# Preparation steps of a three-part kernel: two products between a transfer and its first step, up to five or six steps after a product, twelve working tiles

## Chip, core and metric

The kernel runs on one core of a Trainium2 chip. The metric is the device time of one execution in microseconds (us). The engines are TensorE (PE, with its weight loads PEld), VectorE (DVE), ScalarE (ACT), GpSimd (POOL) and SyncE (SP), whose queue issues the DMA transfers.

## What is computed

Attention over 4 batches, 8 heads, 576 positions and head size 64 gives 2304 tokens of width 512. Two layers with an inner width of 1536 follow; the inputs are fp32, and the weights reach the kernel as 64-bit words.

```python
q_p = phi(q)                                    # phi(x) = max(x, exp(x) - 1) + 1
mem_out = (q_p @ M_prev) / (q_p . z_prev + 1e-6)
local = softmax(causal(q @ k.T * scale)) @ v
g = 1 / (1 + exp(-beta))
x = (g * mem_out + (1 - g) * local)             # -> [2304, 512]
gate = 1 / (1 + exp(-(x @ w_gate)))             # layer 0
x = (gate * (x @ w_val)) @ w_out
out = ((x @ w_a) * (x @ w_b)) @ w_out2          # layer 1
```

## The kernel before

**Products.** Each fp32 operand is split into a rounded high part and a low part. A product is three TensorE passes, high·high, high·low and low·high (`mm3`, L447 to L452; in `out_rows` of layer 1, L1178 to L1180). Tokens form four blocks of 512 columns (0 to 3) and one short block of 256 (block `B` = 4). The inner width is 12 chunks of 128 columns, `c`.

**Order of the work.** Attention takes the first 337 us. Block 3 and the short block then pass through the first four chunks (`early`: per chunk a gate product `tg`, a value product `tv`, `gate()`, and an out product in `flush`). After it, for each layer, the pairs of chunks in `PAIRS` (4 in layer 0, 6 in layer 1): `group(layer, g, 0)`, `plain` (the short block), `group(layer, g, 1)`; then `outs(layer)`. A group multiplies two chunks with two blocks in seven products instead of eight, in the order 1, 2, 6, 5, 7, 3, 4. Each is 12 matmuls of 128x512 for each of two kinds of weights, in two PSUM banks. Three products add into banks of an earlier one, after ACT has copied these out (`keep`, L1038): product 6 into those of 1, product 7 into those of 6, product 3 into those of 5. In this part PE runs in the order in which the code is written; a scheduler orders the other engines.

**Preparation.** After each product `hook(rate)` raises the count of turns and gives up to `rate` steps to the first `WIN` unfinished tasks of one list (`steps`). A step starts only if its working tiles (`t`, NT of 128x512), staging buffers (`s`, NS of 512 KB) and units (NL and NH places for finished operands) are free. The tasks are:

- `piece`: load one chunk of weights into staging `st` (SP, L815/L819); two ACT steps that scale (L827, L828); two DVE steps that shift and merge (L830, L833); a POOL add into `wt` (L838), which frees the staging; then, unless the chunk is mixed first, the high part on ACT (L806) and the low part on DVE or POOL (L800);
- `mix` and `convert`: sums of two chunks, then their high and low parts;
- `x_mixed` and `x_plain`: the same for the tokens of two blocks, or of the short one.

In `outs`, `g_split` loads one block and chunk of the gated product back (L1159) and splits it on ACT (L1161) and DVE or POOL (L1162), three blocks and chunks ahead of its product. In `early`, `gate()` multiplies on DVE (L531), rounds on ACT (`gh`, L148) and subtracts on DVE (`gl`, L538).

Of the kernel before, what the change touches and what calls it, by code (L numbers as in the profile page):

```python
# [13 lines left out]
I32 = mybir.dt.int32  # L14
# [5 lines left out]
def kernel(  # L20
# [17 lines left out]
    P = 128  # L38
# [490 lines left out]
    def gate(vps, s, n, tag="g"):  # L529

        st["gate"] = vec.tensor_tensor(  # L531
            out=s[:, 0:n], in0=vps[:, 0:n], in1=s[:, 0:n], op=ALU.mult
        )
        te = (dict(tag="gh", bufs=NG), dict(tag="gl", bufs=NG)) if NE is None else 2 * (dict(tag="e", bufs=NE),)
        gh = work.tile([P, 512], F32R, name="gh", **te[0])
        gl = work.tile([P, 512], F32R, name="gl", **te[1])
        rnd(gh[:, 0:n], s[:, 0:n], "g" in CD)
        (pool if NE is None else vec).tensor_tensor(  # L538
            out=gl[:, 0:n], in0=s[:, 0:n], in1=gh[:, 0:n].bitcast(F32), op=ALU.subtract
        )  # L540
        return gh, gl
# [197 lines left out]
    with tc.manual_schedule(engines={mybir.EngineType.PE}):  # L739
# [3 lines left out]
        work = bctx.enter_context(tc.tile_pool(name="workb", bufs=2))  # L743
        NL, NH, NE, NT, NS = 15, 10, 7, 10, 2
        wl = bctx.enter_context(tc.tile_pool(name="wl", bufs=NL))
# [31 lines left out]

        def units_left(half):
            return sum(h[2] - h[1] for h in homes if half in (h[3], "A"))

# [28 lines left out]
        def piece(layer, c, kind, half, mixed, on_pool):  # L809
            yield (0, 0, 1)  # L810
            free["s"] -= 1
            s = stp.tile([P, 512, 2], I32, tag="st", name="st")
            w32 = src[layer][kind].bitcast(I32)
# [4 lines left out]
            else:  # L818
# [3 lines left out]
                )  # L822
            yield (0, 1, 0)
            hi, lo = s[:, :, 1], s[:, :, 0]
# [11 lines left out]
            )  # L836
            yield (0, 0, 0)
            pool.tensor_tensor(out=c32, in0=c32, in1=lo, op=ALU.add)  # L838
            freed.append("s")
            if mixed:  # L840
# [46 lines left out]
        def x_mixed(layer, sb, j):  # L887
# [14 lines left out]

            yield ("L", 0, 0)
            high(1, a11)
# [30 lines left out]
        def x_plain(layer):  # L935
# [24 lines left out]

            yield ("L", 0, 0)
            a = [high(kk) for kk in (0, 1)]
# [10 lines left out]
        def task(gen, when=None):  # L973
            tasks.append([gen, None, when])

        def advance(x):
            x[1] = next(x[0], False)
            if x[1] is False:
                tasks.remove(x)

        WIN = 5

        def steps(k):

            starved, seen = False, 0
            for x in list(tasks):
                if x[2] is not None:
                    if not x[2]():
                        starved = True
                        continue  # L990
                    x[2] = None
                seen += 1
                if not k or seen > WIN:
                    break
                if x[1] is None:
                    x[1] = next(x[0])
                u, t, s = x[1]
                if starved and (u or t):
                    continue
                if u and not units_left(u) or t > free["t"] or s > free["s"]:  # L1000
                    starved = True
                    continue
                advance(x)
                k -= 1
# [12 lines left out]
        def need(f):  # L1017

            for n in range(200):
                if f():  # L1020
                    return
                hook(3)
            raise AssertionError(f"no progress {units_left()} {free} {[(x[0].__name__, x[0].gi_frame.f_locals.get('layer'), x[0].gi_frame.f_locals.get('sb'), x[0].gi_frame.f_locals.get('c'), x[0].gi_frame.f_locals.get('kind'), x[1]) for x in tasks[:10]]}")

# [106 lines left out]
        def plain(layer, g, rate):  # L1131

            n = cols(B)
            last_g = g == PAIRS[layer][-1][0]
            for c in (g, g + MATE[layer]):
                need(lambda: (layer, KD - 1) in x4 and all((layer, c, k) in ws for k in H2))
                o = []
# [17 lines left out]
        def g_split(layer, blk, c):  # L1155
# [5 lines left out]
            act.activation(out=t[:, 0, 0:n], in_=f, func=AF.Copy)  # L1161
            (vec if c % 2 and not layer else pool).tensor_tensor(  # L1162
                out=t[:, 1, 0:n], in0=f, in1=t[:, 0, 0:n].bitcast(F32), op=ALU.subtract
# [22 lines left out]
        def outs(layer, rate):  # L1186
# [3 lines left out]
            for m, (blk, c) in enumerate(seq):  # L1190
                while ahead < min(m + 4, len(seq)):
                    settle_free()
                    key = (layer, seq[ahead][1], 2)
                    need(lambda: key in ws and units_left(half_of(ws[key])))
                    g_split(layer, *seq[ahead])
                    ahead += 1
# [117 lines left out]
        for c in upper:  # L1314
            task(piece(0, c, 2, "A", False, False))
        wave(1, 0, False)
# [7 lines left out]
        for c in every:  # L1324
            task(piece(1, c, 2, "A", False, False))

        ends = []
        early(B - 1, 3)
        early(B, 3)
        for layer in H2:  # L1330
            for g, h in PAIRS[layer]:
                group(layer, g, 0, 3)
                plain(layer, g, 3)
                group(layer, g, 1, 3)
            outs(layer, 3)
        bctx.close()
# [31 lines left out]
```

## Time and profile before

| | before |
|---|---|
| median of 3 runs | 1119.66 us (1119.29 to 1122.21) |
| profiled execution | 1121.79 us, span 1120.0 us |
| PE, DVE, ACT, POOL busy | 95%, 55%, 50%, 44% |

The profile is of one execution; its times count from the start of the span. Busy shares are means over the span. In brackets a row gives the idle time of the engine before it and what ended that. PEclk is the TensorE clock that was granted, as a share of full speed (2.4 GHz).

### The profile page before, as it was taken

What the parts mean: (1) busy time and instruction counts of PE and PEld (TensorE: products, weight loads), DVE (VectorE), ACT (ScalarE), POOL (GpSimd) and SP (SyncE); (2) the same over time, 40 slices, a digit from 0 to 9 for tenths busy, and PEclk for the clock granted to TensorE, in tenths of its full rate; (3) what the DMA queues carried; (4) which work ended last, traced back from release to release, by engine and by line L of the source; (5) the groups of instructions that cost most, each with busy time, mean ns of one, the idle gap of its engine ahead of it and who ended that gap; (6) DMA issues with size and microseconds to landing.
All of it is one profiled execution on the core that took longest, in us unless ns stands there. A gap on an engine that the chain in (4) does not pass through costs nothing. (4 is left out here: it accounts for less than half of the span.)

```text
span 1120.0 us, 16371 instructions
## 1 busy us (share of the span) xinstructions
PE 1065.5 (95%) x5624; PEld 848.9 (76%) x5624; DVE 616.8 (55%) x1179; ACT 557.3 (50%) x1173; POOL 492.2 (44%) x432
## 2 busy tenths in 40 slices
PE   5888999999999889999999999989999999989998
PEld 3556677777777777888888878768888888868886
DVE  3888755555434785456459574956555455550000
ACT  4877766666644454454555342534344444442221
POOL 1566552242121553444446451643453444764542
PEclk8999999999999999999999999989999999999999
DMA  6565533323114333323248756313323323742343
GB/s 148 135 166 152 141 92 105 82 69 101 41 67 124 107 110 122 104 85 132 79 157 291 239 197 221 113 58 122 112 87 123 107 82 132 245 142 89 107 137 100
DMA packets 147204, 140.63 MB, mean 126 GB/s; under 512 B 73776, under 2 KB 107696, under 8 KB 147120
## 3 DMA queue, kind: packets, MB, share of 16 engines
q1 hardware_dynamic: 147120, 139.58, 39.5%
q8 instruction: 44, 0.72, 0.3%
q14 instruction: 40, 0.33, 0.1%
HBM read 97.00 MB, written 42.54 MB: 125 GB/s over the span
## 5 line engine op out<-in xcount | busy, mean ns | idle before, releaser
L450 PE MATMUL gv<-xm,w 128*128 128x512 f32 (+1 forms) x752 | 275.0, 366 | 3.5 <-DVE w L800 3.5
L448 PE MATMUL gv<-xm,w 128*128 128x512 f32 (+1 forms) x752 | 274.8, 365 | 3.6 <-ACT ev L1038 3.6
L449 PE MATMUL gv<-xm,w 128*128 128x512 f32 (+1 forms) x752 | 274.6, 365 | 0.0
L448 PEld LDWEIGHTS gv<-xm,w 128*128 128x128 f32 x752 | 143.1, 190 | 27.8 <-ACT ev L1038 4.9
L450 PEld LDWEIGHTS gv<-xm,w 128*128 128x128 f32 x752 | 142.9, 190 | 26.6 <-DVE w L800 4.0
L449 PEld LDWEIGHTS gv<-xm,w 128*128 128x128 f32 x752 | 143.1, 190 | 22.8
L1038 ACT ACTIVATE ev<-gv 128x512 f32<-128x512 f32 (+1 forms) x168 | 92.7, 562 | 127.7 <-PE gv L450 127.4
L1042 DVE TENSOR_TENSOR ev<-gv,ev 128x512 f32<-128x512 f32 x120 | 82.2, 689 | 119.1 <-PE gv L450 87.2
L1162 POOL TENSOR_TENSOR gs<-ev,gs 128x512 fp32r<-128x512 f32 (+1 forms) x80 | 99.8, 1263 | 96.3 <-ACT gs L1161 96.1
L1047 POOL TENSOR_TENSOR ev<-ev 128x512 f32<-128x512 f32 x60 | 84.9, 1415 | 127.9 <-DVE ev L1042 52.2
L838 POOL TENSOR_TENSOR wt<-wt,st 128x512 int32<-128x512 int32 x60 | 84.6, 1417 | 92.8 <-DVE wt L833 67.8
L1161 ACT ACTIVATE gs<-ev 128x512 fp32r<-128x512 f32 (+1 forms) x100 | 55.8, 583 | 89.5 <-DMA ev<-gd 65.1
L1180 PE MATMUL gv<-w,gs 128*128 128x512 f32 x216 | 85.4, 395 | 2.9 <-POOL gs L1162 2.9
L1179 PE MATMUL gv<-w,gs 128*128 128x512 f32 x216 | 85.1, 394 | 0.8 <-DVE w L800 0.8
L1178 PE MATMUL gv<-w,gs 128*128 128x512 f32 x216 | 84.8, 392 | 0.1
L228 ACT ACTIVATE s<-s,mx 128x320 f32<-128x320 f32 (+3 forms) x128 | 77.5, 607 | 6.5 <-DVE mx L223 6.5
L148 ACT ACTIVATE aw<-tp 128x512 f32<-128x512 f32 (+2 forms) x112 | 56.2, 513 | 43.3 <-PE tp L329 34.7
L223 DVE CUSTOM_DVE_ANT_0 s<-sc,mask 64x64 f32<-64x64 f32 (+4 forms) x160 | 68.8, 480 | 15.7 <-PE sc L194 15.7
L827 ACT ACTIVATE wt<-st 128x512 f32<-128x512 f32 x60 | 40.0, 669 | 71.1 <-DMA st<-in_moe_w_out_dram 23.9
L800 POOL TENSOR_TENSOR w<-mx,w 128x512 fp32r<-128x512 f32 x40 | 53.8, 1361 | 44.3 <-ACT w L806 44.0
L233 POOL COPY mix<-s 128x128 f32<-128x128 f32 x64 | 21.5, 338 | 109.9 <-ACT s L228 109.9
L1239 DVE COPY ev<-gv 128x512 f32<-128x512 f32 x9 | 6.2, 691 | 114.2 <-PE gv L1180 114.2
(137 smaller groups left out, 2105.9 us busy)
## 6 DMA issues: line engine op xcount, KB each, us to landing
gd<-ev SPq DMA_DIRECT2D x80, 256.0 KB
ev<-gd SPq DMA_DIRECT2D x80, 256.0 KB
st<-in_moe_w_out_dram SPq DMA_DIRECT2D x24, 512.0 KB
st<-in_moe_w_gate_dram SPq DMA_DIRECT2D x12, 512.0 KB
st<-in_moe_w_val_dram SPq DMA_DIRECT2D x12, 512.0 KB
st<-in_moe_w_a_dram SPq DMA_DIRECT2D x12, 512.0 KB
st<-in_moe_w_b_dram SPq DMA_DIRECT2D x12, 512.0 KB
x<-rd SPq DMA_DIRECT2D x32, 144.0 KB
```

What stands on the lines that cost most here:

```text
L228: act.activation(out=o, in_=s, func=AF.Exp, scale=-1.0, bias=mx[0:m, i:i + 1], accum_out=sms[p % 2][0:m, i:i + 1, e],)
L448: pe.matmul(o, lhsT=w[:, 0, ws_], rhs=xh, start=first, stop=False, skip_group_check=True)
L449: pe.matmul(o, lhsT=w[:, 0, ws_], rhs=xl, start=False, stop=False, skip_group_check=True)
L450: return pe.matmul(o, lhsT=w[:, 1, ws_], rhs=xh, start=False, stop=last, skip_group_check=True)
L838: pool.tensor_tensor(out=c32, in0=c32, in1=lo, op=ALU.add)
L1038: act.activation(out=t[:, 0:n], in_=src[:, 0:n], func=func)
L1042: st["gate"] = vec.tensor_tensor(out=t, in0=src, in1=t, op=ALU.add)
L1047: pool.tensor_tensor(out=ts[0], in0=ts[0], in1=ts[1], op=ALU.mult)
L1162: (vec if c % 2 and not layer else pool).tensor_tensor(out=t[:, 1, 0:n], in0=f, in1=t[:, 0, 0:n].bitcast(F32), op=ALU.subtract)
L1178: pe.matmul(o, lhsT=t[:, 0, r], rhs=w[:, 0], start=first, stop=False)
L1179: pe.matmul(o, lhsT=t[:, 0, r], rhs=w[:, 1], start=False, stop=False)
L1180: st["gate"] = pe.matmul(o, lhsT=t[:, 1, r], rhs=w[:, 0], start=False, stop=last)
```

## The change

It changes when preparation steps are issued, on which engine a few of them run, and one place in the order of products.

- A step can name a number of turns since the task's last step. The first step behind a transfer names two (`piece`, `x_mixed`, `x_plain`). The list looks at 7 tasks instead of 5.
- In pieces that are not mixed, the DVE steps and the POOL add are one step.
- NT goes from 10 to 12, NL from 15 to 14. Out weights of layer 1 may be loaded into a spare unit when no staging is free (more than four units left), and go to alternating halves.
- The rates are 4 and 2 in `early` (both were 3), 5 in the first and the last pair of each layer, 6 in `outs(1)`; 3 elsewhere.
- `gl` of block 3 in `early` goes from DVE to POOL; the low parts of `g_split` in layer 1 go from POOL to DVE. `g_split` runs one further ahead where a unit is free.
- In layer 0 the short block's chunks 4 and 8 come ahead of the first group.

```diff
-        (pool if NE is None else vec).tensor_tensor(
+        (pool if NE is None or n == 512 else vec).tensor_tensor(
             out=gl[:, 0:n], in0=s[:, 0:n], in1=gh[:, 0:n].bitcast(F32), op=ALU.subtract
-        NL, NH, NE, NT, NS = 15, 10, 7, 10, 2
+        NL, NH, NE, NT, NS = 14, 10, 7, 12, 2
...
         def units_left(half):
+            if half == "S":
+                return free["s"] or units_left("A") > 4
...
         def piece(layer, c, kind, half, mixed, on_pool):
-            yield (0, 0, 1)
-            free["s"] -= 1
-            s = stp.tile([P, 512, 2], I32, tag="st", name="st")
+            spare = not mixed and layer
+            yield ("S" if spare else 0, 0, not spare)
+            staged = None
+            if free["s"]:
+                free["s"] -= 1
+                s = stp.tile([P, 512, 2], I32, tag="st", name="st")
+            else:
+                staged = take("st", "A")
...
-            yield (0, 1, 0)
+            yield (0, 1, 0, 2)
...
-            yield (0, 0, 0)
+            if mixed:
+                yield (0, 0, 0)
             pool.tensor_tensor(out=c32, in0=c32, in1=lo, op=ALU.add)
-            freed.append("s")
+            if staged is None:
+                freed.append("s")
+            else:
+                drop(staged)
...
-            yield ("L", 0, 0)
+            yield ("L", 0, 0, 2)
             high(1, a11)
...
-            yield ("L", 0, 0)
+            yield ("L", 0, 0, 2)
             a = [high(kk) for kk in (0, 1)]
...
-        WIN = 5
+        WIN = 7
...
-                u, t, s = x[1]
+                u, t, s, *d = x[1]
+                if d and turn_[0] < x[3] + d[0]:
+                    starved = starved or bool(u)
+                    continue
...
             for c in (g, g + MATE[layer]):
+                if ends and c != g:
+                    ends.pop(0)()
...
-            (vec if c % 2 and not layer else pool).tensor_tensor(
+            (vec if c % 2 or layer else pool).tensor_tensor(
...
-                while ahead < min(m + 4, len(seq)):
+                while ahead < min(m + 5, len(seq)):
                     settle_free()
                     key = (layer, seq[ahead][1], 2)
+                    if ahead > m + 2 and not (key in ws and units_left(half_of(ws[key]))):
+                        break
...
-            task(piece(1, c, 2, "A", False, False))
+            task(piece(1, c, 2, "LH"[c % 2], False, False))
...
-        early(B - 1, 3)
-        early(B, 3)
+        early(B - 1, 4)
+        early(B, 2)
         for layer in H2:
             for g, h in PAIRS[layer]:
-                group(layer, g, 0, 3)
-                plain(layer, g, 3)
-                group(layer, g, 1, 3)
-            outs(layer, 3)
+                rate = 5 if (g, h) in (PAIRS[layer][0], PAIRS[layer][-1]) else 3
+                if g == MA and not layer:
+                    plain(layer, g, 3)
+                    group(layer, g, 0, rate)
+                else:
+                    group(layer, g, 0, rate)
+                    plain(layer, g, rate)
+                group(layer, g, 1, rate)
+            outs(layer, 6 if layer else 3)
```

The order of the engines shows what this moves. Line numbers of the changed kernel are higher: L800 becomes L802, L806 L808, L827 L837, L838 L849, L1038 L1055.

First ACT's queue around the last `keep` of block 3 in `early` (the gate product of chunk 3 is `gv_4243` before and `gv_4242` now). Before:

```order
L148 ACTIVATE gh_4212<-ev_4187 128x512 [waits DVE_49]
L806 ACTIVATE xm_4238<-xt_4139 128x512 [waits DVE_49]
L806 ACTIVATE xm_4260<-xt_4143 128x512
L806 ACTIVATE w_4403<-wt_4170 128x512 [waits Pool_49]
L1038 ACTIVATE ev_4257<-gv_4243 128x512 [waits PE_49]
L806 ACTIVATE xm_4285<-xt_4145 128x512 [waits DMAHW4_49,PE_49]
```

Now:

```order
L148 ACTIVATE gh_4205<-ev_4178 128x512 [waits DVE_49,Pool_49]
L808 ACTIVATE xm_4234<-xt_4054 128x512 [waits DVE_49]
L808 ACTIVATE xm_4237<-s1_4144 128x512
L808 ACTIVATE xm_4260<-xt_4136 128x512 [waits DVE_49]
L1055 ACTIVATE ev_4256<-gv_4242 128x512 [waits PE_49]
L808 ACTIVATE xm_4284<-xt_4140 128x512 [waits PE_49]
L808 ACTIVATE xm_4300<-xt_4142 128x512 [waits DMAHW4_49,PE_49]
L808 ACTIVATE w_4418<-wt_4186 128x512 [waits Pool_49]
L148 ACTIVATE gh_4279<-ev_4256 128x512 [waits DVE_49]
```

The high part of a weight piece, which waits for POOL's add, moved from the place ahead of the `keep` to one behind it, ahead of the last `gh`.

Next POOL's queue at the same place, where `gl` is new. Before:

```order
L800 TENSOR_TENSOR xm_4191<-xt_4058,xm_4191 128x512 [waits DMAHW0_49,Activation_49]
L800 TENSOR_TENSOR xm_4238<-xt_4139,xm_4238 128x512 [waits Activation_49]
L838 TENSOR_TENSOR wt_4170<-wt_4170,st_4061 128x512 [waits DVE_49]
L838 TENSOR_TENSOR wt_4240<-wt_4240,st_4086 128x512 [waits DVE_49,Pool_49]
L800 TENSOR_TENSOR xm_4285<-xt_4145,xm_4285 128x512 [waits DMAHW4_49,Activation_49]
```

Now:

```order
L538 TENSOR_TENSOR gl_4206<-ev_4178,gh_4205 128x512 [waits Activation_49]
L802 TENSOR_TENSOR xm_4260<-xt_4136,xm_4260 128x512 [waits Activation_49]
L849 TENSOR_TENSOR wt_4186<-wt_4186,st_4061 128x512 [waits DMAHW7_49,DMAHW5_49,DVE_49]
L849 TENSOR_TENSOR wt_4189<-wt_4189,st_4063 128x512 [waits DMAHW3_49,DMAHW4_49,DMAHW1_49,DVE_49]
L802 TENSOR_TENSOR xm_4300<-xt_4142,xm_4300 128x512 [waits DMAHW4_49,Activation_49]
L538 TENSOR_TENSOR gl_4280<-ev_4256,gh_4279 128x512 [waits Activation_49,Pool_49]
```

The last `gl` stands behind two adds and one low part.

Last ACT's queue at the start of layer 1's groups, where staged weights (L827/L837, L828/L838) stand between copies out of PSUM (L1038/L1055). Before:

```order
L827 ACTIVATE wt<-st 128x512 [waits DMAHW2_49]
L828 ACTIVATE st<-st 128x512 [waits DVE_49,Activation_49]
L806 ACTIVATE xm<-xt 128x512 [waits DVE_49]
L1038 ACTIVATE ev<-gv 128x512 [waits PE_49]
L806 ACTIVATE w<-wt 128x512 [waits Pool_49]
L1038 ACTIVATE ev<-gv 128x512 [waits DMAHW6_49,PE_49]
L827 ACTIVATE wt<-st 128x512 [waits DMAHW4_49]
L828 ACTIVATE st<-st 128x512 [waits DVE_49,Activation_49]
L1038 ACTIVATE ev<-gv 128x512 [waits DMAHW7_49,PE_49]
```

Now:

```order
L808 ACTIVATE w<-wt 128x512 [waits Pool_49]
L837 ACTIVATE wt<-st 128x512 [waits DMAHW3_49,Activation_49]
L838 ACTIVATE st<-st 128x512 [waits DVE_49,Activation_49]
L1055 ACTIVATE ev<-gv 128x512 [waits PE_49]
L837 ACTIVATE wt<-st 128x512 [waits DMAHW4_49]
L838 ACTIVATE st<-st 128x512 [waits DVE_49,Activation_49]
L808 ACTIVATE xm<-xt 128x512 [waits DVE_49]
L1055 ACTIVATE ev<-gv 128x512 [waits DMAHW7_49,PE_49]
```

The pieces still stand between the copies, but two products behind the issue of their loads instead of one.

## Rows read from the trace of the kernel before

**Rows 1.** Windows of 40 us: busy us (x instructions) by engine, then PEclk, DMA share, GB/s.

```profile
360.00:400.00 40.00, 33.52 (x183) 29.09 (x182) 32.89 (x46) 21.39 (x42) 23.14 (x14) 0.91 0.40 132
440.00:480.00 40.00, 38.06 (x183) 31.90 (x182) 19.92 (x30) 19.23 (x34) 18.13 (x14) 0.96 0.25 88
720.00:760.00 40.00, 35.69 (x145) 28.63 (x146) 24.36 (x33) 14.32 (x26) 18.50 (x14) 0.91 0.23 82
...
960.00:1000.00 40.00, 36.17 (x147) 27.75 (x146) 25.21 (x21) 17.94 (x31) 32.77 (x23) 0.96 0.51 168
```

**Rows 2.** PE's waits from 345 us on: total us, times, longest us.

```profile
PE gv L449 <- DVE gl L538: 4.7, 4, 2.3
PE gv L448 <- ACT ev L1038: 3.6, 3, 1.9
PE gv L450 <- DVE w L800: 3.5, 1, 3.5
PE gv L448 <- ACT gh L148: 2.9, 1, 2.9
PE gv L1180 <- POOL gs L1162: 2.9, 3, 1.9
PE gv L449 <- DVE gs L1162: 2.0, 1, 2.0
PE gv L1179 <- DVE w L800: 0.8, 1, 0.8
```

**Rows 3.** PE's timeline in `early`: start us, length us, instruction.

```profile
371.78 0.50 PE L449 MATMUL gv<-gl,w 128*128 128x512 f32 x1 [1.02 <-DVE gl L538]
372.12 0.39 PE L450 MATMUL gv<-gh,w 128*128 128x512 f32 x1
372.35 0.40 PE L448 MATMUL gv<-gh,w 128*128 128x512 f32 x1
...
382.41 0.63 PE L450 MATMUL gv<-gh,w 128*128 128x512 f32 x1
382.83 0.63 PE L448 MATMUL gv<-gh,w 128*128 128x512 f32 x1
```

**Rows 4.** ACT's timeline in `early` and in both layers' groups.

```profile
374.78 0.63 ACT L806 ACTIVATE w<-wt 128x512 fp32r<-128x512 f32 x1 [4.61 <-POOL wt L838]
375.31 0.58 ACT L1038 ACTIVATE ev<-gv 128x512 f32<-128x512 f32 x1
...
441.42 0.68 ACT L827 ACTIVATE wt<-st 128x512 f32<-128x512 f32 x1 [1.69 <-DMA st<-in_moe_w_val_dram]
...
724.80 0.66 ACT L827 ACTIVATE wt<-st 128x512 f32<-128x512 f32 x1 [2.49 <-DMA st<-in_moe_w_b_dram]
...
732.21 0.68 ACT L828 ACTIVATE st<-st 128x512 int32<-128x512 uint32 x1 [2.68 <-DMA st<-in_moe_w_b_dram]
```

**Rows 5.** DVE's timeline in `early`: the same low part, twice.

```profile
361.06 1.78 DVE L800 TENSOR_TENSOR xm<-xt,xm 128x512 fp32r<-128x512 f32 x1
...
366.17 0.68 DVE L800 TENSOR_TENSOR xm<-xt,xm 128x512 fp32r<-128x512 f32 x1
```

**Rows 6.** POOL's timeline in `early` and at the start of `outs(1)`.

```profile
360.52 5.18 POOL L800 TENSOR_TENSOR xm<-xt,xm 128x512 fp32r<-128x512 f32 x3 [2.67 <-ACT xm L806]
...
983.53 6.09 POOL L1162 TENSOR_TENSOR gs<-ev,gs 128x512 fp32r<-128x512 f32 x4
```

**Rows 7.** The chain that ended last: start us, us, a load's way from issue to landing.

```profile
714.26 3.73 DMA st<-in_moe_w_a_dram
...
963.26 5.45 DMA st<-in_moe_w_out_dram
```

**Rows 8.** Groups by line and form from 345 us on: busy us, mean ns.

```profile
L838 POOL TENSOR_TENSOR wt<-wt,st 128x512 int32<-128x512 int32 x60 | 84.6, 1417 | 92.8 <-DVE wt L833 67.8 <-ACT ev L1038 12.5 <-DMA gd<-ev 3.9
L827 ACT ACTIVATE wt<-st 128x512 f32<-128x512 f32 x60 | 40.0, 669 | 71.1 <-DMA st<-in_moe_w_out_dram 23.9 <-DMA st<-in_moe_w_b_dram 17.0 <-DMA st<-in_moe_w_a_dram 12.8
L806 ACT ACTIVATE w<-wt 128x512 fp32r<-128x512 f32 x60 | 37.5, 629 | 41.9 <-POOL wt L838 39.4 <-PE gv L450 1.7
```

More of the change, by code (lines that the diff above doesn't have):

```diff
@@ L809, in piece @@
         def piece(layer, c, kind, half, mixed, on_pool):
-            yield (0, 0, 1)
-            free["s"] -= 1
-            s = stp.tile([P, 512, 2], I32, tag="st", name="st")
+            spare = not mixed and layer
[6 more added lines that the diff above has]
+                staged = take("st", "A")
+                s = staged.rearrange("p a b -> p (a b)").bitcast(I32).rearrange(
+                    "p (f t) -> p f t", t=2
+                )
             w32 = src[layer][kind].bitcast(I32)
@@ L973, in task @@
         def task(gen, when=None):
-            tasks.append([gen, None, when])
+            tasks.append([gen, None, when, 0])
         def advance(x):
-            x[1] = next(x[0], False)
+            x[1], x[3] = next(x[0], False), turn_[0]
             if x[1] is False:
                 tasks.remove(x)
-        WIN = 5
+        WIN = 7
         def steps(k):
@@ L1022, in need @@
                 hook(3)
-            raise AssertionError(f"no progress {units_left()} {free} {[(x[0].__name__, x[0].gi_frame.f_locals.get('layer'), x[0].gi_frame.f_locals.get('sb'), x[0].gi_frame.f_locals.get('c'), x[0].gi_frame.f_locals.get('kind'), x[1]) for x in tasks[:10]]}")
+            raise AssertionError(f"no progress {units_left("L")} {units_left("H")} {free} {[(x[0].__name__, x[0].gi_frame.f_locals.get('layer'), x[0].gi_frame.f_locals.get('sb'), x[0].gi_frame.f_locals.get('c'), x[0].gi_frame.f_locals.get('kind'), x[1]) for x in tasks[:10]]}")
         def ev():
@@ L1314 @@
         for c in upper:
-            task(piece(0, c, 2, "A", False, False))
+            task(piece(0, c, 2, "LH"[c % 2], False, False))
         wave(1, 0, False)
```

## The prediction

> **What bounds the kernel now.** I began with the page: PE is busy for 95% of the span, and every matmul stays. Its count and shapes are the same before and after; only the place of one stretch moves. So PE's own work can't shrink, and the time can fall only by what PE loses now. Three views give that loss.
>
> The first is the table of PE's waits from 345 us on, behind the attention part, which the change leaves alone [rows 2]. Its rows add up to 4.7 + 3.6 + 3.5 + 2.9 + 2.9 + 2.0 + 0.8 = 20.4 us, in 14 waits. The reader should see that no row names one engine as slow: ACT, DVE and POOL are each late now and then.
>
> The second is the table of windows [rows 1]. In the four windows that hold the longer waits PE's granted clock is 0.91, 0.96, 0.91 and 0.96. The timeline of `early` shows what that is: a 128x512 matmul starts 0.23 us behind the one before it (372.12 to 372.35), and 0.42 us some 2 us after a long wait (382.41 to 382.83) [rows 3]. That is the lower of the clock's two levels, 1.2 instead of 2.4 GHz, for a few us after PE stood still. The loss is 0.09, 0.04, 0.09 and 0.04 of 40 us: 3.6 + 1.6 + 3.6 + 1.6 = 10.4 us.
>
> The third is the timeline at one wait [rows 3]. A wait is counted from the modelled end of the last matmul, which overlaps its successor by 0.39 - 0.23 = 0.16 us, and the first start after it takes 0.34 instead of 0.23 us. Each wait thus costs 0.27 us beyond its row: 14 x 0.27 = 3.8 us.
>
> Together 34.6 us: without any loss the kernel would take 1119.66 - 34.6 = 1085 us. That is the floor, whatever the change does in preparation.
>
> **The change, part by part.** I give each place its wait and its clock, and ask what is left of both.
>
> *Block 3 in `early`, 360 to 400 us.* The loss is 4.7 (`gl`) + 2.9 (`gh`) + 3.6 (clock) = 11.2 us. Its cause is on ACT: the high part of a weight piece waited 4.61 us for POOL's add at 374.78, and the `keep` of the last gate product stood behind it at 375.31 [rows 4]. `gh` and `gl` come from that. The new order puts this `keep` ahead of the high part, so the 2.9 us go. But the last `gl` now stands on POOL, behind two adds at 1.4 us [rows 8] and a low part. On POOL a subtract of this size took 5.18 / 3 = 1.7 us, on DVE 0.68 [rows 5, 6]. I take one add and the longer subtract as late, 1.4 + 1.3 = 2.7 us. The clock then drops once instead of twice, 1.7 us; the short block's two tight places I set at half of nothing to 1.8, 0.9. Left: 5.3. Saved: 5.9. Bounds: nothing left (11.2 saved), or all of it left because POOL is as late as before (0 saved).
>
> DVE's row speaks for caution here. The same low part took 1.78 us at 361.06, while POOL ran three of its own, and 0.68 us at 366.17 [rows 5, 6]. Four subtracts on POOL that overlap DVE would hold DVE for up to 4 x 1.1 = 4.4 us, in a window in which DVE is busy for 32.89 of 40 us [rows 1]. The Trainium skill says so as a rule (SBUF — State Buffer, section "Who interferes with whom"): a DVE instruction with two inputs in SBUF and a GpSimd instruction that reads SBUF exclude each other, and the later one is fully blocked. The rows agree with it in size. By that rule alone the time would be 4.4 us more, 1100 us, still inside the forecast's own range; I keep the sum without it, since most of what DVE does there has a product or more to spare.
>
> *First group of layer 0, about 443 us.* 1.9 + 1.6 (clock) = 3.5 us. ACT waited 1.69 us at 441.42 for a load of weights [rows 4], and the copies out of PSUM that PE needed stood behind. A load took 3.73 to 5.45 us from issue to landing [rows 7]; its first step came one product, 12 x 0.23 = 2.8 us, after it. With two products, 5.5 us, it has landed. Left 0.3. Saved 3.2; bounds 0 and 3.5.
>
> *`outs(0)`, 662 us.* 2.0 us for one split on DVE behind preparation of tokens. Splits now run one further ahead where a unit is free, 2.8 us earlier. Left 0.5. Saved 1.5; bounds 0 and 2.0.
>
> *First group of layer 1, 718 to 744 us.* 1.7 + 3.5 (the low part of a weight) + 3.6 (clock) = 8.8 us, the dearest place. ACT waited 2.49 us at 724.80 and 2.68 us at 732.21 for loads [rows 4]; all that followed was late by that, up to the low part at PE's front. A load of 3.73 us against 5.5 us of gap leaves nothing, if SP issues it at once. Left 1.0, since the load is issued behind POOL's add that frees the staging. Saved 7.8; bounds 0 and 8.8.
>
> *Start of `outs(1)`, 985 to 995 us.* 2.9 + 0.8 + 1.6 (clock) = 5.3 us. POOL is busy for 32.77 of 40 us [rows 1]: four splits took it 6.09 us at 983.53 [rows 6], and the adds of the last out weights stood between. These splits go to DVE, and the spare staging and the rates let all twelve out weights be prepared before the last group ends; by the new order POOL's queue ends with adds and the gating of the last products, and no split stands in it. Left 0. Saved 5.3; the bound below is 0.
>
> *Waits that vanish.* About ten of 14, 10 x 0.27 = 2.7 us more.
>
> *What the rates cost.* Five steps after a product put more ACT work ahead of a copy that PE waits for. A piece takes ACT 2 x 0.669 + 0.629 = 1.97 us [rows 8], so twelve in the last groups of layer 1 take 23.6 us of about 44; a copy has one product, 2.8 us, before PE needs its banks. Two pieces whose two scaling steps meet take 4 x 0.669 = 2.7 us, just that. Bounds: nothing, or as much as the two places of this kind lose now, 8.8 + 3.5 = 12.3 us. I take 2.5, near the lower end, because most products have fewer than five steps ready and the twelve pieces are spread over 14 products.
>
> The rest is priced at nothing. Twelve working tiles and a window of 7 only let steps start. The moved chunks 4 and 8 are the same 48 matmuls of 256 columns; their cover is the out product of `early`, and if a weight is late there, it is the wait of the first group come earlier. Merging DVE's and POOL's step moves the add one product forward.
>
> Sum: 5.9 + 3.2 + 1.5 + 7.8 + 5.3 + 2.7 - 2.5 = 23.9 us. The profiled execution took 1121.79 us, 2.1 more than the median; its sum is 1097.9, and against the median 1119.66 - 23.9 = 1095.8. **Forecast: 1096 us**, and 1091 to 1101 for this case alone.
>
> **The rivals.**
>
> *`gl` on POOL is in time.* `early` then keeps next to none of its 5.3 us, with the two waits' 0.5: 1090 us. For it speaks that POOL is busy for only 23.14 of 40 us there [rows 1]; against it the two adds that stand ahead.
>
> *The gap is eaten, or the rates make waits of their own.* SP issues a load only when POOL's add has freed the staging, and the two turns count from the step in the program, not from that. If the issue is 2 us late, a load of 3.73 us still ends behind 5.5 us, and the places at 443 and 718 us keep their 11 us: 1107. If instead the dense stretches cost the bound of 12.3, it is 1096 + 9.8 = 1106. For it speaks that an add was 4.61 us late for ACT at 374.78 [rows 4]; against it that PE lost only at these two places of many loads.
>
> *It changes nothing that PE waits for*: new waits of the same size elsewhere, 1116 to 1123. Only a coincidence of prices speaks for it.
>
> *Slower.* The loads into spare units stand in SP's one queue. A unit is free in the program when PE's last reader is written, not when it has run; such a load waits for PE, and the stores of products, whose seven buffers the copies need, wait behind it. Twelve loads at one product each, 12 x 2.8 = 33.6 us, less 23.9: 1129. It decides from 23.9 / 12 = 2.0 us held per load. Against it: none of PE's waits now is put down to a store or a buffer that one holds [rows 2], though the stores share SP's queue with all loads.
>
> **How the numbers follow.** Forecast 0.54; `gl` in time 0.12; gap eaten or dense waits 0.24; nothing 0.04; slower 0.06. A measurement here tells about 0.3%, 3.4 us, from no change. All of the first three are faster by more: 0.90. Same 0.04, slower 0.06. The range holds the forecast's case, two thirds of the second and most of the third: 1088 to 1110.
>
> **What would show it.** Right: the row of ACT's `keep` out of the table of PE's waits, DVE's `w` too; POOL's row at the start of `outs(1)` gone, with DVE doing the splits; granted clock 0.99 or more in the windows at 720 and 960 us, and below 1 still between 360 and 400 us, with PE's longest wait there on POOL's `gl`. ACT's waits for loads of weights fall from 2 to 3 us each to below 1. Wrong: PE waits for copies in the last groups of layer 1 (the dense steps), ACT's waits for loads stay (the gap is eaten), or the stores' own queue waits reach PE (slower).

## The result and the profile after

The changed kernel takes 1126.72 us in the median of 6 runs (1125.82 to 1129.70), the kernel before 1119.53 us: 1.0067 times the time, interval 1.0049 to 1.0084. It is slower by 0.67%, where 2% faster was forecast, and outside the range of 1088 to 1110. The profiled execution took 1125.97 us, its span is 1124.2 us; before it was 1120.0. The two profiles thus differ by 4.2 us and the medians by 7.2; what follows explains the 4.2.

Windows of the changed kernel: busy us by engine, then PEclk, DMA share, GB/s.

```profile
360.00:400.00 40.00, 36.61 (x222) 32.47 (x221) 31.00 (x45) 25.13 (x49) 25.68 (x18) 0.96 0.39 132
...
640.00:680.00 40.00, 36.91 (x171) 30.88 (x170) 27.66 (x31) 13.70 (x28) 19.47 (x14) 0.93 0.47 156
...
720.00:760.00 40.00, 38.90 (x193) 32.48 (x192) 25.89 (x35) 17.29 (x33) 18.81 (x13) 1.00 0.32 110
...
760.00:940.00 180.00, 172.92 (x834) 143.88 (x834) 98.85 (x149) 79.05 (x142) 82.06 (x58) 1.00 0.34 116
...
960.00:1000.00 40.00, 36.24 (x151) 29.11 (x151) 21.30 (x28) 12.00 (x20) 6.31 (x4) 0.96 0.33 105
```

The first, third and last answer to [rows 1]: PE is busier at 360 and 720 us, and POOL at 960 us has 6.31 instead of 32.77 us of work. The fourth stretch, the middle of the pairs of layer 1, lost nothing in the kernel before:

```profile
760.00:940.00 180.00, 180.00 (x900) 153.11 (x899) 99.38 (x152) 77.56 (x136) 77.42 (x58) 1.00 0.31 109
```

PE's waits in the changed kernel from 345 us on answer to [rows 2]: total us, times, longest us.

```profile
PE gv L448 <- ACT ev L1055: 12.6, 10, 3.0
PE gv L448 <- DVE ev L1059: 3.8, 1, 3.8
PE gv L448 <- ACT gs L1180: 2.9, 1, 2.9
PE gv L449 <- POOL gl L538: 2.5, 1, 2.5
PE gv L450 <- DVE w L802: 1.1, 1, 1.1
PE gv L448 <- ACT gh L148: 0.6, 1, 0.6
PE gv L449 <- DVE gl L538: 0.3, 1, 0.3
PE gv L449 <- POOL gs L1181: 0.2, 1, 0.2
```

The rows that the change was to remove are gone or small (`gh`, `w`, `gs` on POOL). In their place stand waits for copies out of PSUM: 12.6 us instead of 3.6. By place, waits and clock together, before and after (the timeline splits the 12.6 us into 3.7 in layer 0 and 8.9 in layer 1, of which 7.1 lie between 760 and 940 us and 1.8 in the last group):

| place | before | after | forecast left |
|---|---|---|---|
| first part, 360 to 400 us | 11.2 | 5.0 | 5.3 |
| first group of layer 0 | 3.5 | 3.7 | 0.3 |
| `outs(0)` | 2.3 | 6.3 | 0.5 |
| first group of layer 1 | 8.8 | 1.1 | 1.0 |
| its pairs from 760 to 940 us | 0 | 7.1 | 0 |
| its last group, from 942 us | 0 | 7.2 | 2.5, for all dense stretches |
| start of `outs(1)` | 5.3 | 0 | 0 |
| sum | 31.1 | 30.4 | 9.6 |

(The names of the places are the prediction's; by the timeline its first groups are the second group of the layer's first pair, in layer 1 with the start of the next. `outs(0)` before has a wait of 0.3 us for a split on POOL at 640.68 us, the eighth row of the table of waits, which [rows 2] leave out; after, the lower clock behind its wait reaches past 680 us, where PEclk is 0.99.) So the sum of PE's losses is nearly as large as before: 0.7 us less, and 0.5 us more for 17 waits instead of 15, at 0.27 each. The 4.2 us that the span grew lie mostly in something else: the matmuls of the out products follow each other more slowly. In `outs(1)` 36 chunks of 12 matmuls on end, 432, all but without a wait, run from 999.94 to 1098.16 us before and from 1002.34 to 1102.06 us after, the starts of the first and of the one behind the last:

```profile
999.94 0.39 PE L1178 MATMUL gv<-w,gs 128*128 128x512 f32 x1
...
1098.16 0.39 PE L1178 MATMUL gv<-w,gs 128*128 128x512 f32 x1
```

```profile
1002.34 0.40 PE L1197 MATMUL gv<-w,gs 128*128 128x512 f32 x1
...
1102.06 0.40 PE L1197 MATMUL gv<-w,gs 128*128 128x512 f32 x1
```

That is 0.2274 us each before and 0.2308 after, at a granted clock of 1.00 in both. Over the 648 matmuls of `outs(1)` it is 2.2 us, and over the 384 of 512 columns in `outs(0)` about 1.2 (0.2278 us each before, 0.2308 after); about 1 us is not assigned.

**One of the new waits, from end to end.** A product of a group is 12 matmuls for both kinds of weights together, six for each, in 2.73 us; the text ahead of the prediction can be read as twice that. In the fourth pair of layer 1 the second group starts at 853.02 us before and at 850.32 us after (the first 128x512 matmul behind the short block). Before, two adds on POOL free the two staging buffers just ahead of it, and the loads go out:

```profile
852.28 2.91 POOL L838 TENSOR_TENSOR wt<-wt,st 128x512 int32<-128x512 int32 x2 [5.45 <-ACT ev L1038]
```

```profile
853.95 0.38 SPq L819 DMA_DIRECT2D st<-in_moe_w_a_dram  x1
...
855.21 0.38 SPq L819 DMA_DIRECT2D st<-in_moe_w_b_dram  x1
```

```profile
857.79 0.67 ACT L827 ACTIVATE wt<-st 128x512 f32<-128x512 f32 x1 [1.23 <-DMA st<-in_moe_w_a_dram]
...
860.99 1.07 ACT L1038 ACTIVATE ev<-gv 128x512 f32<-128x512 f32 x2
```

ACT waits 1.23 us for the load and makes the copy at 860.99, when the third product has just ended (853.02 + 3 x 2.73 = 861.2). After:

```profile
854.01 2.91 POOL L849 TENSOR_TENSOR wt<-wt,st 128x512 int32<-128x512 int32 x2 [6.98 <-DVE wt L843]
```

```profile
859.31 0.68 ACT L837 ACTIVATE wt<-st 128x512 f32<-128x512 f32 x1 [5.45 <-DMA st<-in_moe_w_a_dram]
...
860.45 0.59 ACT L1055 ACTIVATE ev<-gv 128x512 f32<-128x512 f32 x1
862.29 0.66 ACT L837 ACTIVATE wt<-st 128x512 f32<-128x512 f32 x1 [1.25 <-DMA st<-in_moe_w_b_dram]
...
863.39 1.07 ACT L1055 ACTIVATE ev<-gv 128x512 f32<-128x512 f32 x2
```

```profile
864.02 0.51 PE L448 MATMUL gv<-xm,w 128*128 128x512 f32 x1 [1.19 <-ACT ev L1055]
```

Against the group's start the adds moved from 0.7 us ahead of it to 3.7 us behind it, 4.4 us later. ACT's first step on the next load stands where it stood, ahead of the same copy, and now waits 5.45 us. The third product's two copies are due at about 857 and 858.5, as its two halves end; they come at 860.45 and 863.39, and PE stands for the second. Three of the other pairs show the same, at 767, 814 and 905 us: ACT waits 6.19, 6.25 and 5.29 us for one load and 1.43, 1.29 and 1.80 us for the next, ahead of the copies. ACT's queue in the program shows that the step is not held back. The numbers in the names rise in the order in which the program is written, and `wt_8674` stands ahead of `ev_8492`:

```
L1055 ACTIVATE ev_8447<-gv_8440 128x512
L1055 ACTIVATE ev_8456<-gv_8449 128x512
L837 ACTIVATE wt_8674<-st_8636 128x512
L838 ACTIVATE st_8636<-st_8636 128x512
L1055 ACTIVATE ev_8492<-gv_8440 128x512
L837 ACTIVATE wt_8677<-st_8638 128x512
L838 ACTIVATE st_8638<-st_8638 128x512
L1055 ACTIVATE ev_8500<-gv_8449 128x512
```

The reason is in the code: `hook` issues the steps with `tc.issue_after(st["gate"].ins)`, which queues them behind that instruction, and in the groups the gate is a DVE instruction. What a step puts on DVE is queued behind it; its ACT instructions, as this order shows, go where the scheduler likes.

### The profile page after: what moved, and what is told of

It reads as the page before. It is cut to its first block, busy times and chain, and to the rows that moved or that the text cites. A ratio compares the mean times of both kernels' runs of the same rounds, so it can differ in the third digit from the quotient of the medians.

```text
span 1124.2 us, 16315 instructions
## 1 busy us (share of the span) xinstructions
PE 1067.8 (95%) x5624; PEld 847.6 (75%) x5624; DVE 645.1 (57%) x1235; ACT 553.8 (49%) x1173; POOL 431.3 (38%) x376
## 5 line engine op out<-in xcount | busy, mean ns | idle before, releaser
L448 PE MATMUL gv<-xm,w 128*128 128x512 f32 (+1 forms) x752 | 274.5, 365 | 16.5 <-ACT ev L1055 12.6
L1064 POOL TENSOR_TENSOR ev<-ev 128x512 f32<-128x512 f32 x60 | 87.4, 1457 | 117.6 <-DVE ev L1059 63.6
L1055 ACT ACTIVATE ev<-gv 128x512 f32<-128x512 f32 (+1 forms) x168 | 90.3, 560 | 70.6 <-PE gv L450 70.3
L849 POOL TENSOR_TENSOR wt<-wt,st 128x512 int32<-128x512 int32 x60 | 87.4, 1465 | 92.5 <-DVE wt L843 81.5
L1181 DVE TENSOR_TENSOR gs<-ev,gs 128x512 fp32r<-128x512 f32 (+1 forms) x80 | 55.6, 713 | 49.3 <-ACT gs L1180 48.7
L837 ACT ACTIVATE wt<-st 128x512 f32<-128x512 f32 x60 | 39.5, 668 | 86.3 <-DMA st<-in_moe_w_a_dram 30.0
L802 POOL TENSOR_TENSOR w<-mx,w 128x512 fp32r<-128x512 f32 x40 | 56.3, 1428 | 51.6 <-ACT w L808 51.5
L808 ACT ACTIVATE w<-wt 128x512 fp32r<-128x512 f32 x60 | 37.4, 629 | 67.5 <-POOL wt L849 65.6
L802 DVE TENSOR_TENSOR w<-wt,w 128x512 fp32r<-128x512 f32 x60 | 62.8, 1059 | 7.0 <-ACT w L808 6.8
```

The source lines that it names most:

```text
L448: pe.matmul(o, lhsT=w[:, 0, ws_], rhs=xh, start=first, stop=False, skip_group_check=True)
L802: (pool if on_pool else vec).tensor_tensor(out=t[:, 1], in0=f, in1=t[:, 0].bitcast(F32), op=ALU.subtract)
L1055: act.activation(out=t[:, 0:n], in_=src[:, 0:n], func=func)
L1064: pool.tensor_tensor(out=ts[0], in0=ts[0], in1=ts[1], op=ALU.mult)
```

## The experiments

Times are medians; the ratio, with its interval, is to the kernel before on the same chip. The changed kernel's own is 1.0067 (1.0049 to 1.0084). The runs lie on three chips (e1 to e8, e9 to e12, e13 to e15), so runs of different ones are compared by their ratios.

| | base, edit | us | ratio |
|---|---|---|---|
| e1 | changed, no gap in pieces | 1118.33 | 0.9984 (0.9971 to 0.9998) |
| e2 | changed, ACT held | 1116.33 | 0.9966 (0.9955 to 0.9977) |
| e3 | changed, out weights in any half | 1121.82 | 1.0010 (0.9996 to 1.0024) |
| e4 | before, splits on DVE | 1114.98 | 0.9949 (0.9930 to 0.9968) |
| e5 | e2 and e3 | 1111.06 | 0.9897 (0.9866 to 0.9928) |
| e6 | changed, rate 3 in last pair | 1129.00 | 1.0071 (1.0052 to 1.0091) |
| e7 | before, gap alone | 1152.94 | 1.0284 (1.0261 to 1.0307) |
| e8 | before, ACT held | 1115.66 | 0.9961 (0.9945 to 0.9977) |
| e9 | changed, third staging buffer | 1124.19 | 1.0023 (1.0008 to 1.0038) |
| e10 | changed, `gl` on DVE | 1129.27 | 1.0076 (1.0053 to 1.0099) |
| e11 | e5 without gap | 1118.64 | 0.9982 (0.9961 to 1.0002) |
| e12 | before, e4 and e8 | 1110.77 | 0.9911 (0.9885 to 0.9937) |
| e13 | e12 and three parts | 1109.44 | 0.9893 (0.9876 to 0.9909) |
| e14 | e13, ACT not held | 1117.75 | 0.9967 (0.9950 to 0.9985) |
| e15 | changed, splits three ahead | 1136.37 | 1.0141 (1.0121 to 1.0160) |

**The gap: e1, e7, e9.**

```diff
-            yield (0, 1, 0, 2)
+            yield (0, 1, 0)
```

> The changed kernel without the two turns in the pieces. Theory 1 (late staging): a turn holds back only the DVE steps; ACT's first step stands ahead of the same copies as before, while DVE's step, POOL's add and with them the next load come one product later. Then the waits of PE for copies by ACT (12.6 us in 10 waits) fall below 4, those between 760 and 960 us go, and the time is about 1116. Theory 2 (density): the window of 7, twelve tiles and the rates pile up steps, whatever the gap. Then these waits stay above 8 us and the time within 2 us of 1126.7.

The middle of the pairs of layer 1 is whole again:

```profile
760.00:940.00 180.00, 180.00 (x885) 152.46 (x885) 100.68 (x153) 81.42 (x142) 82.03 (x59) 1.00 0.33 114
```

The time came near the expected 1116, but the waits for copies fell only to 9.2 us instead of below 4, so density has a part too. Those of the last group, whose rate is five, did not go, and the longest is there:

```profile
950.13 0.50 PE L448 MATMUL gv<-xm,w 128*128 128x512 f32 x1 [2.64 <-ACT ev L1055]
```

In e7 the kernel before gets the two turns in its pieces, the lines of `advance` and `steps` that count them, and the places that they need:

```diff
-            yield (0, 1, 0)
+            yield (0, 1, 0, 2)
...
-        NL, NH, NE, NT, NS = 15, 10, 7, 10, 2
+        NL, NH, NE, NT, NS = 14, 10, 7, 12, 2
```

> The kernel before with the two turns in the pieces alone (and twelve tiles, fourteen low units, which it needs). Theory 1 (late staging): the waits for copies appear in the pairs of layer 1, where the kernel before has none between 750 and 960 us, 1 to 3 us for each pair: 6 us or more there in all, and the first groups' waits at 443 and 720 us do not shrink by more than half. Rival: the gap does its work and needs the other parts for nothing; no wait appears between 750 and 960 us and those at 443 and 720 us go.

2.8% slower. PE loses 7.6 us in the stretch, and the clock falls to 0.98; the waits are for the low part of a weight, not for copies as expected:

```profile
760.00:940.00 180.00, 172.39 (x832) 144.61 (x831) 95.15 (x137) 66.65 (x118) 71.24 (x51) 0.98 0.29 97
```

```profile
PE gv L450 <- DVE w L800: 13.3, 5, 3.1
PE gv L448 <- ACT ev L1041: 7.4, 6, 3.4
```

That is a part of the 33 us only: PE also waits 15.0 us for splits in the two `outs`, where the table of waits before has 5.2. So the gap has no one price: 33 us alone, 8 to 9 us within the change (e1). In the pair shown above it put the staging off by 4.4 us; that the same delay is what makes the weights late here is argued, not shown.

```diff
-        NL, NH, NE, NT, NS = 14, 10, 7, 12, 2
+        NL, NH, NE, NT, NS = 13, 10, 7, 12, 3
...
+        st3, staged_ = bctx.enter_context(tc.tile_pool(name="st3", bufs=1)), [0]
...
-                s = stp.tile([P, 512, 2], I32, tag="st", name="st")
+                staged_[0] += 1
+                s = (st3 if staged_[0] % 3 == 0 else stp).tile([P, 512, 2], I32, tag="st", name="st")
```

> The changed kernel with a third staging buffer and one low unit less; the two turns stay. Theory 1 (late staging): with a third buffer the next load needn't wait for the add that the gap puts off, so the load has landed when its step on ACT stands ahead of a copy; the waits of PE for copies between 760 and 960 us (7 of the 10 waits, 9.5 us) fall below 3 and the time to about 1117. Rival: the waits come from ACT's order or from DVE's load of steps alone, which a buffer doesn't change; they stay above 6 us, and the time within 3 us of 1126.7.

With the gap kept and a buffer more (and one low unit less) the stretch has no loss:

```profile
760.00:940.00 180.00, 180.00 (x895) 152.90 (x894) 98.73 (x149) 80.83 (x144) 77.77 (x58) 1.00 0.33 112
```

So the gap acts through the staging. The time fell by less than expected, since other waits grew: 3.9 us for a split on POOL in `outs(0)`, 2.7 us at 574 to 579 us; the last group still waits 4.7 us for a sum on DVE.

**ACT's order: e2, e8.** In e2 (and in e8 on the kernel before) ACT's steps are held as DVE's are:

```diff
-            act.activation(out=t[:, 0:n], in_=src[:, 0:n], func=func)
+            st["keep"] = act.activation(out=t[:, 0:n], in_=src[:, 0:n], func=func)
...
-            with tc.issue_after(st["gate"].ins):
+            with tc.issue_after(st["gate"].ins), tc.issue_after(st["keep"].ins):
```

> The changed kernel, with every preparation step on ACT queued behind the last copy that the program has written, so that a turn holds back ACT as it does DVE. Theory 1: no load stands ahead of a copy any more, the waits for copies go almost wholly, 12.6 + 10 x 0.27 = 15 us less: 1111 to 1114. Theory 2: ACT's steps then only come later, weights arrive late at PE, and the time is 1124 or more.

> The kernel before with ACT's preparation steps queued behind the last copy, and nothing else. Theory 1: loads stand ahead of copies before the change too; the waits for copies (3.6 us) and what hangs on them at 443 us go, 3.5 us or more: 1116 or less. Rival: the order of ACT's queue costs nothing where the loads are early enough, and the steps that come later make weights late: 1119.5 or more.

e8 held; e2 held in its mechanism, though 1116.33 lies above the 1111 to 1114. In e2 the waits for copies fell from 12.6 to 2.0 us, all in the last group, and the stretch is all but whole:

```profile
PE gv L448 <- ACT ev L1055: 2.0, 2, 1.7
```

```profile
760.00:940.00 180.00, 179.69 (x881) 151.84 (x880) 100.63 (x157) 79.07 (x141) 86.49 (x61) 1.00 0.36 120
```

In e8 no wait for a copy is left, at 443 us or anywhere. The wait for a low part at 727 to 735 us stays (3.8 us); holding ACT doesn't cure it.

**The halves: e3.** Operands lie in two pools of the on-chip memory, a low and a high half. The change puts the out weights of both layers, not of layer 1 alone as the list of changes has it, into the two in turn. Both out-weight tasks are put back:

```diff
-            task(piece(1, c, 2, "LH"[c % 2], False, False))
+            task(piece(1, c, 2, "A", False, False))
```

> The changed kernel with the out weights placed in either half as before, not in alternating halves. Theory 3 (halves): in the out products a matmul starts 0.2308 us behind the last where the chunk before lay in the other half, and 0.227 where it lay in the same; with fewer changes of half the mean falls to 0.2280 or less, 3 us over 1,030 matmuls: 1123.7. Rival: the splits on DVE slow the matmuls by running beside them; the spacing stays at 0.2308 and the time at 1126.7.

432 matmuls of `outs(1)` take 98.53 us (0.2281 each). The gain is larger than expected, since the wait of 2.9 us in `outs(0)` and the slow stretch behind it are not there; some of that is lost again at the end of the last group (4.8 us of wait for 3.8).

**Splits on DVE, alone: e4; with ACT held: e12.**

```diff
-            (vec if c % 2 and not layer else pool).tensor_tensor(
+            (vec if c % 2 or layer else pool).tensor_tensor(
```

> The kernel before with the splits of layer 1 on DVE and nothing else. If POOL's queue of splits was the cause of the waits at 985 to 995 us, they go: 5.3 us and their 0.8 of overlap less, 1113.5. If the adds of the last out weights are the cause, PE waits for a weight in their place and no more than 1 to 2 us are saved: 1118.

> The kernel before with two things alone: ACT's steps queued behind the copies (eighth experiment, 4.5 us) and the splits of layer 1 on DVE (fourth, 6.3 us). If they are apart, the gains add up: 1109. If POOL's relief already took the same waits, no more than 7 us are gained: 1113.

POOL's queue was the cause: 6.3 us in e4, and with e8's 4.5 us the two gains nearly add up (10.1 us in e12). In e4 waits of 0.7 us for a split on ACT and 0.8 us for a low part are left at that place. The spacing in e4 is 0.2274 us (432 matmuls from 992.89 to 1091.11 us): splits on DVE don't slow the matmuls, so that rival of e3 falls.

**Together: e5, and e5 without the gap: e11.**

> The second experiment's queueing of ACT and the third's placing of the out weights together. If the causes are apart, the gains add up: from the second kernel's 1116.3 the 3 us of slower matmuls and the 5 to 6 us of the wait at 668 to 676 us go, 1108. If the wait at 668 us comes from the one split that is loaded further ahead and not from the halves, it stays and only 3 us are gained: 1113.

> The fifth experiment without the two turns in the pieces. Theory 1: with ACT queued behind the copies the gap has no use left and only frees the staging late; the wait for a weight at 724 to 731 us (5.2 us with its clock) falls by half or more: 1108 or less. Rival: with ACT held, the gap keeps loads off the copies; without it the waits for copies rise by 3 us or more: 1114.

e5 gained, less than the full sum. e11 went the other way: the wait for a weight at 724 us did go, but waits of 1.5 to 3.2 us for splits and of 2.7 and 2.3 us for a sum came elsewhere. The waits for copies did not rise (2.8 us, 3.6 in e5), so the rival's reason is not borne out either. With ACT held, the kernel with the gap is 0.9% faster than the one without, by the ratios; why is open.

**Rate: e6.** Three steps in the last pair of layer 1:

```diff
-                rate = 5 if (g, h) in (PAIRS[layer][0], PAIRS[layer][-1]) else 3
+                rate = 5 if (g, h) in (PAIRS[layer][0], PAIRS[layer][-1]) and (layer, g) != (1, 5) else 3
```

> The changed kernel with three instead of five steps in the last pair of layer 1. Density: DVE's queue there has three weight pieces ahead of the sums that PE waits for; with three steps the waits from 945 to 968 us (7.7 us with what follows them) go and 6 us are gained, 1120.5, unless the out weights are late: then PE waits for them at the start of the out products, as before the change, and the time stays within 2 us of 1126.7.

The waits from 945 to 968 us went, and the out products waited for splits instead:

```profile
PE gv L1199 <- DVE gs L1181: 2.8, 2, 1.5
PE gv L1197 <- ACT gs L1180: 2.8, 1, 2.8
```

The rate of 5 gives back about what it costs, and the start of `outs(1)` owes its freedom from waits to that rate too, not to the splits on DVE alone.

**`gl`: e10.**

```diff
-        (pool if NE is None or n == 512 else vec).tensor_tensor(
+        (pool if NE is None else vec).tensor_tensor(
```

> The changed kernel with the gl of block 3 back on DVE. If POOL's place of the last gl is the cause of what is left in the first part (2.5 us of wait, then the lower clock, 5.7 us between 376 and 397 us), 3 us or more go: 1123.5 or less. If DVE, which is busy for 31 of 40 us there, is then late with gl as it was before, the waits for gl add up to 2.5 us or more again and the time is 1126.7 or more.

The time is the changed kernel's within the intervals. Block 3's wait for `gl` (2.5 us on POOL) is gone, but the short block's, on DVE in both kernels, grew from 0.3 to 2.1 us; neither side of the expectation is borne out clearly.

**The fourth split: e15.**

```diff
-                while ahead < min(m + 5, len(seq)):
+                while ahead < min(m + 4, len(seq)):
```

> The changed kernel with splits three ahead instead of four. If the wait at 671 to 679 us (6.2 us with the slow matmuls of 256 columns behind it) comes from the fourth split, whose load takes a buffer and a place in the queue ahead of the one that PE needs, it goes: 1121. If it comes from the halves, whose placing by the third experiment took it away, it stays and the time is within 2 us of 1126.7.

Slower by 0.7% than the changed kernel, by the ratios: `outs(0)` now waits 6.4 us for one split on ACT. The fourth split is a help, not the cause.

**Parts on the kernel before: e13, e14.** Rates 4 and 2 in `early`, `gl` on POOL, the fourth split, splits on DVE.

> The twelfth experiment with three parts of the change added: the rates 4 and 2 and gl on POOL in the first part, and splits one further ahead. No gap, no rate of 5, no alternating halves. If these parts are worth what the changed kernel showed at their places, the first part loses 5.5 instead of 11 us and the wait at 655 us (4.9 us) goes: 1111 - 10 = 1101. If what they gained there came from the gap, the time stays within 3 us of 1110.8.

> The same without the queueing of ACT: the change without its gap, its rates of 5, its merged step, its halves and its tiles. If the gap and what belongs to it are the whole cause of the loss, this is faster than the kernel before by the terms that held, 6.3 + 5.5 us and more: 1107. If the other parts make waits of their own, 1113 or more.

e13, e5 and e12 are the fastest, 1.1%, 1.0% and 0.9% below the kernel before, and their intervals overlap. So against e12 the parts brought nothing that shows, where 10 us were expected: the first part still waits 3.5 us for `gl` on POOL, 1.4 for `gl` on DVE and 1.2 for `gh`. In e14, with ACT free, PE waits 4.3 us for one `gh`.

## Why the prediction was wrong

**The step that failed** is the price of the gap: "With two products, 5.5 us, it has landed." It takes the count of turns as a distance between a load and its first step on ACT. There is no such distance: a turn holds only DVE's steps, while ACT's stand where the scheduler puts them. What the two turns do move is DVE's step, and with it POOL's add, the free staging and the next load: 4.4 us later against the products in the pair shown. The rows of ACT's order ahead of the prediction show the pieces between the copies as before; the sentence behind them, "two products behind the issue of their loads", was read off the program's text, and no time bore it out. The rival "the gap is eaten" named the staging as the weak point, but priced it only where PE already waited, at 443 and 718 us. Its price lay where PE had not waited: 7.1 us between 760 and 940 us, in pairs that the forecast left at nothing (e1, e2 and e9 each take it away, by three ways; e7 makes a like loss out of the kernel before, there as waits for weights). ACT's waits for loads, which were to fall below 1 us, rose to 5 and 6 us in these pairs.

For the profiled execution the prediction's sum is 1097.9; it took 1125.97, 28.1 us more. Of these, 20.8 are losses (30.4 left instead of 9.6): 7.1 in the pairs, 4.7 in the last group, 5.8 in `outs(0)`, 3.4 in the first group of layer 0, and 0.2 less elsewhere. The overlap of 17 waits instead of the four that were to stay is 3.5, the halves are 3.4, and 0.4 is open. (Against the median the miss is 30.9 us: the profile before lay 2.1 us above its median, the one after 0.75 below.)

**First part:** right. 5.0 us left for 5.3 forecast, with the last `gl` on POOL as the wait (2.5 us for 2.7). DVE was busy for 31.00 us there instead of 32.89, so the 4.4 us that the caution set beside the sum did not come. That `gl` on DVE would do worse or better is not shown (e10).

**First group of layer 0:** wrong; 3.7 us left instead of 0.3. The gap did not keep the loads off the copies: ACT waits 3.16 us for a load at 438.23, ahead of a copy. Holding ACT removes the wait for copies (e2; 0.9 us for a sum is left). It is not the gap that makes it: 2.5 us stay without the gap (e1), 3.1 with a third buffer (e9).

**`outs(0)`:** wrong; 6.3 instead of 0.5. The fourth split helps (e15), and the new wait was absent with the out weights in any half (e3, e5), but came back in e11, which has that placing too. What brings it stays open.

**First group of layer 1:** 1.1 us left for 1.0. The size was right, the reason not shown to be the gap: e1 has no gap in its pieces and waits 0.9 and 1.3 us for copies and 1.4 us for a sum between 700 and 750 us, so the larger part of the gain came without it. Which of tiles, window and rate brought it is open; no run takes these, the merged step or the moved chunks 4 and 8 away alone.

**Start of `outs(1)`:** right; e4 shows the larger part of the cause alone, and e6 that the rate has a part.

**Rates:** the second term that failed: 2.5 us were taken for all dense stretches, and the last group alone cost 7.2, inside the bound of 12.3. The mechanism was half right. Copies by ACT were late, as forecast, for 1.8 us; the larger loss is on DVE, which the term left out. At the end of the last group a sum that PE needs stands on DVE behind the steps of several weights, some lengthened beside POOL's adds, and PE waits 3.8 us:

```profile
958.46 2.40 DVE L843 SCALAR_TENSOR_TENSOR wt<-st,wt 128x512 int32<-128x512 int32 x2
960.78 3.46 DVE L802 TENSOR_TENSOR w<-wt,w 128x512 fp32r<-128x512 f32 x2
964.17 1.28 DVE L1059 TENSOR_TENSOR ev<-gv,ev 128x512 f32<-128x512 f32 x2
```

```profile
960.34 3.36 POOL L849 TENSOR_TENSOR wt<-wt,st 128x512 int32<-128x512 int32 x2 [0.63 <-DVE wt L843]
```

A low part takes 3.46 / 2 = 1.7 us there instead of 0.68 [rows 5], with two adds of POOL beside it, 3.36 us from 960.34 on. By the Trainium skill (SBUF — State Buffer, section "Who interferes with whom") such a pair of instructions contends for ports of the memory that one of the two holds at a time. The longer time agrees with that. With the lower clock behind it, 1.6 us, this end of the last group makes 5.4 of the 7.2 us. With three steps a product (e6) all three waits of the group go, and as much is lost at the start of `outs(1)`.

**Not in the sum:** the alternating halves, priced at nothing and not even named: 3.4 us.

**The slower rival** (loads in spare units that hold SP) is not what happened: no wait of PE names a store or a load's place.

## What to carry to other kernels

A delay counted in program steps delays only those engines whose instructions are tied to the count; look in the order, engine by engine, for what is written late and stands early. A gap ahead of the step that frees a shared buffer is paid for by every later user of the buffer, so it is priced over the whole ring and most of all in stretches that have no loss now. A change of where tiles lie is a change of its own, and wants a term.

## What the runs showed of the hardware

A chunk of 12 out matmuls takes 2.72 us when its operands lie in the same half of the memory as those of the chunk before, and 2.76 to 2.78 us when the half changes. In the kernel before only chunk 1 (low, behind a high one) and chunk 4 (high, behind a low one) change; here chunks 0 to 3 of the third block:

```profile
1032.68 0.39 PE L1178 MATMUL gv<-w,gs 128*128 128x512 f32 x1
...
1035.40 0.40 PE L1178 MATMUL gv<-w,gs 128*128 128x512 f32 x1
...
1038.17 0.39 PE L1178 MATMUL gv<-w,gs 128*128 128x512 f32 x1
...
1040.89 0.39 PE L1178 MATMUL gv<-w,gs 128*128 128x512 f32 x1
```

2.72, 2.77 and 2.72 us. In the changed kernel every chunk changes half and takes 2.76 to 2.78. By the addresses of the tiles in the built kernels, the 35 chunks of `outs(1)` before that stay in their half, without a wait, take 2.72 to 2.73 us and the eight that change it 2.76 to 2.77; in e3, e5 and e11 too the slow chunks are those behind a change. Weight and split lie in the same half here, so which of the two matters stays open, as does the reason.

Two loads of 512 KB that went out 1.3 us apart (853.95 and 855.21) reached ACT's first step 3.8 and 4.7 us later (857.79 and 859.87); a load with no other load under way took 3.73 us [rows 7].
